# A three-stage kernel: where the decode pieces, the early weight splits and the sums of added tiles stand

## The chip, the cores and the metric

The kernel runs on one core of a Trainium2 chip. The metric is the device time of one launch in microseconds. Engines are named as in the profile: PE (TensorE matmuls), PEld (its weight loads), DVE (VectorE), ACT (ScalarE), POOL (GpSimd), SP (SyncE, used here for transfers). Every engine runs its own list of instructions in order; the order of that list is fixed when the kernel is built.

## What is computed

```python
def _attn_ref(q, k, v):                  # (2, 8, 1152, 64)
    q_pool = q.reshape(B, H, S // 2, 2, D).mean(axis=3)
    scores = np.matmul(q_pool, k.transpose(0, 1, 3, 2)) / np.sqrt(D)
    attn = softmax(scores)
    return np.matmul(attn, v)

def _moe_ref(x, w_gate, w_output_gate, w1, w2):   # x (1152, 512), 8 experts, width 1024
    e_idx = np.argmax(x @ w_gate, axis=1)
    # each token: relu(x @ w1[e]) @ w2[e], scaled by the gate's probability and an output gate

def _moe2_ref(x, w_in, w_out):           # 512 -> 2048 -> 512
    h = x @ w_in
    return (h * np.tanh(softplus(h))) @ w_out
```

The three are applied one after the other to 1152 tokens, all in float32. The weights of the last layer come as 64-bit values (`wio`) that the kernel turns into float32 itself; this is called decoding below.

## The kernel before

**Attention** (stage 1) works on eight pairs of heads, each in nine steps t = 0 to 8, one step per 128 keys. In step t PE makes scores (`sc`, L257 to L268), ACT makes their exponentials `Pt[p, t]` (tile `pt`, 128 x 1152), PE multiplies with the values into the PSUM tile `pvt` (`pv`, L274). The sums of the exponentials, which softmax needs, are also matmuls into `pvt`: `psums` (L284 to L294) multiplies `Pt` by a matrix of ones, `e2`. To halve these, `add_two` (L280) has DVE add the tiles of two steps into `St[p]` (tile `st`): for t in `twos` = (1, 3, 5) it adds Pt[t-1] and Pt[t], and `psums(p, t)` takes `St`. `add_two(p, t-1)` is issued in step t, as its first task, and the values and sums of step t-1 are issued in step t too (the letter p of the string below).

In the same steps PE also makes the score maxima of the *next* pair (`mx`, L215), and DVE reduces them (`Mp`, L103); three PSUM buffers hold them. The order within a step is written out by hand as a string, "0mmrpsmMt": 0 stands for the scores, m and M for one chunk of maxima, p for the values and `psums` of the step before, and so on. Each m first pops one task from a list (`mxc`, L544ff). The tasks are those that a table puts at that step (`at_step`: splitting keys and queries `klo`, `qlo`, the reciprocals `sum_rec`, outputs `x_out`), with `add_two` ahead of all of them, and a decode piece behind. At the end of step 0 ACT and DVE take the sums of the pair before out of PSUM (`post_evac`, tiles `xu` and `sm`), and the next pair's values wait for that, since there is one `pvt`.

**Decoding** (`decode`, L407ff) turns 32 chunks of `wio` (512 KB each, tile `wraw`) into the float32 tiles `wd`. A chunk has three pieces: piece 0 takes an absolute value on ACT (`dm<-wraw`) and a sign on DVE (`ds<-wraw`); piece 1 clamps on DVE (`dm<-dm`) and joins bits (`ds<-wraw,ds`); piece 2 shifts (`dm<-dm`) and writes the result (`wd<-dm,ds`). Pieces are taken strictly in order. Two `wraw` buffers are loaded ahead; the transfers are issued on SP in attention and on ACT afterwards. `DEC_T` says in which steps of pairs 0 to 6 a piece stands, `DEC_A` how many chunks are decoded in attention; in the last pair each step takes up to three pieces. What is left is spread over the iterations of the three wide experts by `DECS`.

**Experts** (stage 2): eight slots in the order of `slots`, three of them wide (ten iterations each), the others narrow (six each); the third wide one is followed by the two last narrow ones. Each iteration splits weights in two parts (`w1h`/`w2h` on ACT, `w1l`/`w2l` on DVE or POOL) and runs matmuls (L826 to L828); a narrow expert runs plain float32 matmuls (L979, L988, L847) with its `xn`, `hr`, `hn` copies on ACT. Results (`y`) are scattered to `ybuf` by POOL (L858). Beside this, `split_hi` (ACT, `wh<-wd`) and `split_lo` (DVE, `wd<-wd,wh`) begin to split the decoded weights of the last layer: `NPRE` of sixteen are done early, the first ones once all chunks are decoded (L1134ff).

**Hand-over**: `reload` (L869) reads three blocks of `ybuf` back by transfers on ACT's queue, which wait for the scatters; `rescale` (L873) multiplies them on DVE; every engine takes a branch (L1161) behind its part; then `turn` (L877, L879) and `add_rows` (L909) bring them to PE for the **last layer** (stage 3).

The last layer's splits are laid out by a table, `stages`: step 0 has `split_hi` of number 3, step 1 its `split_lo`, and so on to number 15.

Of the kernel before, what the change touches and what calls it, by code (L numbers as in the profile page):

```python
# [23 lines left out]
HQ = SQ // 2  # L24
# [6 lines left out]
KT = S // P  # L31
# [53 lines left out]
def kernel(ctx, tc, cst, qt, kt, v, wgo, w1, w2, wio, out):  # L85
    nc = tc.nc
    V, A, G, T, SP = nc.vector, nc.scalar, nc.gpsimd, nc.tensor, nc.sync
    mm = T.matmul
# [4 lines left out]
    def tt(eng, out, a, b, op):  # L93
        eng.tensor_tensor(out=out, in0=a, in1=b, op=op)  # L94
# [53 lines left out]
    e2 = ap.tile([P, 2, 32], F32, name="e2")  # L148
# [8 lines left out]
    Pt, pvt = {}, {}  # L157
# [17 lines left out]
        SP.dma_start(out=vt[p], in_=v[p])  # L175

    DEC_M = 32
    DEC_T, DEC_A = [1, 3, 5, 7, 8], 19
    tqt = {}

    def qsum(p, h):
# [95 lines left out]
    twos = (1, 3, 5)  # L277
    St = {}

    def add_two(p, t):  # L280
        St[p] = ap.tile([P, 2, SQ], F32, name="st", bufs=1)
        tt(V, St[p], Pt[p, t - 1], Pt[p, t], ALU.add)

    def psums(p, t):  # L284


        if t + 1 in twos:
            return
        src = St[p] if t in twos else Pt[p, t]
        for f in range(2):  # L290
            for h in range(2):
                for a in range(2):
                    q_, t0 = 64 * h + 32 * a, 256 * a + 160 * f
                    mm(pvt[p][q_:q_ + 32, f, HQ:HQ + 160], lhsT=e2[:, h], rhs=src[:, h, t0:t0 + 160], start=False, stop=t == KT - 1, skip_group_check=True)  # L294

    def post_evac(p):
        b, hp = divmod(p, 4)
# [102 lines left out]
    dq, wq = [], []  # L400
# [101 lines left out]
    def raw_ahead(pool, end):  # L502
        while dec[2] < min(dec[0] + 2, end):
            load_raw(dec[2], pool)
            dec[2] += 1
# [15 lines left out]
    for g in range(-9, 9 * NPAIR):  # L521
        p, t = divmod(g, 9)
        if t == 0:
            todo = list(chunks) if p + 1 < NPAIR else []
            mtodo = list(mchunks) if p + 1 < NPAIR else []
        tasks = list(sched.get(g, ()))
        if p >= 0 and t - 1 in twos:
            tasks.insert(0, lambda p=p, t=t: add_two(p, t - 1))
        if p == NPAIR - 1:
            tasks.append(lambda: [(raw_ahead(ap, DEC_A), decode_step(ap, DEC_A)) for _ in range(3)])  # L530
        elif p >= 0 and t in DEC_T:
            tasks.append(lambda: (raw_ahead(ap, DEC_A), decode_step(ap, DEC_A)))

        slot = [0]

        def mxc(todo=todo):
            if tasks:
                tasks.pop(0)()
            if todo:
                max_chunk(p + 1, *todo.pop(0))  # L540
            slot[0] += 1

        prev = divmod(g - 1, 9)
        seq = "0mmrpsmMt" if p < NPAIR - 1 else "0mmrpsmmt"
        if g < 0:
            seq = "mmmm"
            todo += mtodo
            mtodo = []
        assert not (t == 8 and (todo or mtodo)), (p, len(todo), len(mtodo))
        if t < 3:  # L550
            seq = seq.replace("M", "m")
        for ch in seq:
            if ch == "0":
                if p >= 0:
                    scores(p, t)
            elif ch == "m":
                mxc()
            elif ch == "M":
                if mtodo:
                    mxc(mtodo)  # L560
                else:
                    mxc()
            elif ch == "s":
                if p > 0 and t == T_S:
                    sum_log(p - 1)
            elif ch == "t":
                if p > 0 and t == T_T:
                    sum_tr(p - 1)
            elif ch == "e":
                mxc([])  # L570
            elif ch == "r":
                if t == 8 and 0 <= p < NPAIR - 1:
                    max_rows(p + 1)
            elif ch in "pfg" and prev[0] >= 0:
                if ch in "pf":
                    pv(*prev, 0)
                if ch in "pg":
                    pv(*prev, 1)
                    psums(*prev)
        for f in tasks:  # L580
            f()
        if t == 0 and p > 0:
            post_evac(p - 1)
        if p > 0 and t in (T_X - 1, T_X):
            x_tr(p - 1, t - T_X + 1)
        if g == -1:
            warm(6)
        if g == -1:
            max_rows(0)
            warm(2)  # L590
# [445 lines left out]
        return [(lambda i=i: pre(i), lambda i=i: main(i), lambda: None) for i in range(-1, 6)]  # L1036

    NF = FF2 // P
    NPRE = 3
    ws2 = {}  # L1040


    def split_hi(b_, f):
        if b_ == 0:
            pool, n = (wq[0], NPRE) if f < NPRE else (zp, NF - NPRE)
            hi = pool.tile([P, 1024], F32R, name="wh", bufs=n)
# [12 lines left out]
    LATE = 1  # L1059
    XGB = 4  # L1060

    DECS = [[0, 0, 0, 0, 0, 0, 0, 0, 2, 2], [0, 2, 2, 2, 2, 2, 2, 2, 2, 2], [0, 2, 2, 2, 2, 2, 2, 2, 2, 1]]
    RQ = 2
    slots = []
    for pos_ in order:
# [31 lines left out]
    for q, (n_, i, _, main, w_, _) in enumerate(flat):  # L1097
        if i == 0:
            used += len(slots[n_][1])
            if n_ + 1 < len(slots):  # L1100
                load_w(slots[n_ + 1][0], ej, slots[n_ + 1][0])
        if q + 2 < len(flat):
            flat[q + 2][2]()
        if gnext < min(used + 4, len(allc)):
            gather(*allc[gnext])
            gnext += 1
        for f in xpre.pop(-q - 1, ()):
            f()
        main()
        if q + 2 < len(flat):  # L1110
            flat[q + 2][5]()
        if q == RQ:
            routing_rest()
            over = routing_over()
        if RQ < q <= RQ + 4:
            oi = next(over)
        if q == RQ + 5:
            routing_oix(oi)
            T.transpose(pr[:TT, P:2 * P], gsc, ident)
            gt_ = rt("gt", [P])  # L1120
            act(gt_[:TT], pr[:TT, P:2 * P])
            A.dma_start(out=gbuf.rearrange("(t p) o -> t (p o)", p=P), in_=gt_[:TT])
            rstack.close()
            fstack = ExitStack()
            fp.append(fstack.enter_context(tc.tile_pool(name="fps", bufs=1, space=PSUM, side="right", reuse_waits="tile")))
            dstack = ExitStack()
            dq.append(dstack.enter_context(tc.tile_pool(name="dq", bufs=1, side="right", reuse_waits="tile")))
            raw_ahead(dq[0], DEC_M)
        if w_ and q > RQ + 5:
            for _ in range(DECS[slots[n_][0]][i]):  # L1130
                decode_step(dq[0], DEC_M)
            raw_ahead(dq[0], DEC_M)
        if dec[0] == DEC_M and dq and not wq:
            dstack.close()
            wq.append(ctx.enter_context(tc.tile_pool(name="wq", bufs=1, side="right", reuse_waits="tile")))
            q0 = q
        elif wq and (q - q0) % 3 == 0 and len(ws2) < NPRE:
            f = len(ws2)
            split_hi(0, f)
            split_lo(0, f)  # L1140
    assert dec[0] == DEC_M and len(ws2) == NPRE, (dec, len(ws2))

# [158 lines left out]
    for i in range(len(steps) + LAG):  # L1301
# [4 lines left out]
        if i < len(steps):  # L1306
            b_, f = steps[i]
# [49 lines left out]
```

## Time and profile before

| | us |
|---|---|
| runs | 706.27, 703.7, 701.53 (median 703.7) |
| profiled execution | 704.62 |
| its span, first to last instruction | 702.6 |
| PE busy in the span | 649.7 (92%) |
| DVE busy | 521.1 (74%) |
| ACT busy | 369.8 (53%) |
| POOL busy | 138.3 (20%) |

Times in rows are microseconds from the start of the span. By stages: attention 0 to 295.4, routing to 314.3, experts to 449.5 (the third wide one's end), the last two narrow experts and the hand-over to 484.4, the last layer to 702.6. A row of a timeline has the start, the duration, engine, line, operation, tiles with their shapes and a count; in brackets the idle time of the engine just before it and what released it. An L number is a line of the kernel, and where a helper issues all operations (L91, L94, L97, L100, L103) the tile names tell them apart.

### The profile page before, as it was taken

To read this page: it belongs to the slowest core of one execution; us is meant where nothing else is said; L and a number is where in the kernel's file an instruction comes from. 1 tells how busy PE (TensorE), PEld (TensorE's weight loads), DVE (VectorE), ACT (ScalarE), POOL (GpSimd) and SP (SyncE) were. 2 spreads that over 40 slices of the span, in tenths; PEclk is the share of its full clock that TensorE was granted. 3 is DMA by queue.
4 is the path that set the end of the run, shared out by engine and by line. 5 is a ranking of instruction groups with operands and counts; after the bars stand their busy time and mean duration, and the time that the engine had idled before them with its cause. 6 is when DMAs were issued, how large, how long until landed. Compare 5 with 4: busy or idle time off the path is not lost. (4 is left out here: it accounts for less than half of the span.)

```text
span 702.6 us, 11490 instructions
## 1 busy us (share of the span) xinstructions
PE 649.7 (92%) x4335; PEld 503.0 (72%) x4335; DVE 521.1 (74%) x1034; ACT 369.8 (53%) x752; POOL 138.3 (20%) x139
## 2 busy tenths in 40 slices
PE   4999999999999999859989999968899999999997
PEld 3766767666667666438877968638787899999995
DVE  6896969787787978556554848732999977897775
ACT  6556575656565646324245535433666554555543
POOL 5300000000000000034023323201322332233322
PEclk9999999999999999979999999998999999999999
DMA  6854544344442113158489778851000020001001
GB/s 226 281 144 119 132 131 112 114 114 130 114 132 84 64 47 131 41 163 327 172 309 354 263 261 315 302 209 46 0 1 1 1 91 1 0 1 46 1 0 45
DMA packets 26641, 88.33 MB, mean 126 GB/s; under 512 B 2886, under 2 KB 7631, under 8 KB 22482
## 3 DMA queue, kind: packets, MB, share of 16 engines
q1 hardware_dynamic: 20688, 71.13, 29.2%
q0 software_dynamic: 3568, 8.79, 5.6%
q10 hardware_dynamic: 2322, 7.61, 3.1%
q8 instruction: 35, 0.57, 0.3%
q14 instruction: 28, 0.23, 0.1%
HBM read 79.65 MB, written 8.39 MB: 125 GB/s over the span
## 5 line engine op out<-in xcount | busy, mean ns | idle before, releaser
L91 ACT ACTIVATE pt<-sc 128x320 f32<-128x320 f32 (+1 forms) x216 | 96.5, 488 | 66.9 <-PE sc L259 59.8
L103 DVE TENSOR_REDUCE Mp<-mx 128x1 f32<-128x384 f32 x198 | 102.9, 548 | 37.4 <-PE mx L215 36.3
L100 POOL TENSOR_SCALAR u<-u 128x384 f32<-128x384 f32 x48 | 60.6, 1263 | 153.1 <-ACT u L91 132.3
L274 PE MATMUL pv<-pt,vt 128*64 128x288 f32 x576 | 86.8, 422 | 1.0 <-DVE sm L94 0.5
L215 PE MATMUL mx<-at,qs 128*128 128x384 f32 x176 | 57.3, 383 | 10.4 <-DVE qs L97 8.4
L826 PE MATMUL zps<-yh,wh 128*128 128x384 f32 x188 | 64.0, 341 | 1.7 <-DVE n L97 1.7
L828 PE MATMUL zps<-yl,wh 128*128 128x384 f32 x188 | 63.3, 337 | 0.0
L827 PE MATMUL zps<-yh,wd 128*128 128x384 f32 x180 | 60.8, 338 | 0.0
L1266 PE MATMUL ops<-wh,gl 128*128 128x512 f32 x144 | 57.7, 403 | 3.0 <-DVE gl L94 2.4
L274 PEld LDWEIGHTS pv<-pt,vt 128*64 128x64 f32 x576 | 35.7, 137 | 31.8 <-issue 15.1
L1266 PE MATMUL ops<-wh,gh 128*128 128x512 f32 x144 | 56.9, 395 | 0.2 <-ACT gh L91 0.2
L215 PEld LDWEIGHTS mx<-at,qs 128*128 128x128 f32 x176 | 31.3, 195 | 31.1 <-issue 11.3
L1266 PE MATMUL ops<-wd,gh 128*128 128x512 f32 x135 | 53.1, 394 | 0.0
L91 ACT ACTIVATE l<-n,two 128x384 f32<-128x384 f32 x48 | 29.5, 615 | 25.0 <-DVE n L97 25.0
L97 DVE SCALAR_TENSOR_TENSOR l<-n,r 128x384 f32<-128x384 f32 x48 | 26.6, 555 | 19.1 <-ACT r L91 19.1
L91 ACT ACTIVATE u<-zps 128x384 f32<-128x384 f32 x48 | 23.2, 484 | 33.1 <-PE zps L828 29.7
L826 PEld LDWEIGHTS zps<-yh,wh 128*128 128x128 f32 x188 | 35.4, 188 | 3.7 <-ACT r L91 2.0
L1266 PEld LDWEIGHTS ops<-wh,gl 128*128 128x128 f32 x144 | 27.0, 188 | 14.0 <-DVE gl L94 7.0
L91 ACT ACTIVATE gh<-n 128x384 fp32r<-128x384 f32 x48 | 24.8, 517 | 20.6 <-DVE n L97 20.4
L828 PEld LDWEIGHTS zps<-yl,wh 128*128 128x128 f32 x188 | 35.3, 188 | 0.0
L100 DVE TENSOR_SCALAR dm<-dm 128x512 f32<-128x512 f32 x64 | 29.7, 464 | 7.4 <-ACT dm L91 7.3
L91 ACT ACTIVATE dm<-wraw 128x512 f32<-128x512 f32 x32 | 21.7, 678 | 25.0 <-DMA wraw<-in_wio 17.0
(276 smaller groups left out, 1593.0 us busy)
## 6 DMA issues: line engine op xcount, KB each, us to landing
wt<-in_w SPq DMA_DIRECT2D x32, 1024.0 KB, 7.1
wraw<-in_wio SPq DMA_DIRECT2D x19, 512.0 KB, 4.7
kd<-in_kt SPq DMA_DIRECT2D x16, 576.0 KB, 3.8
wraw<-in_wio ACTq DMA_DIRECT2D x13, 512.0 KB, 6.9
vt<-in_v SPq DMA_DIRECT2D x8, 576.0 KB, 7.1
tq<-in_qt SPq DMA_DIRECT2D x12, 288.0 KB, 6.3
tq<-in_qt POOLq DMA_DIRECT2D x12, 288.0 KB, 4.5
pt<-in_qt SPq DMA_DIRECT2D x4, 576.0 KB, 3.9
```

The source lines that it names most:

```text
L91: A.activation(out=out, in_=in_, func=func, **kw)
L97: V.scalar_tensor_tensor(out=out, in0=a, scalar=s, in1=b, op0=op0, op1=op1)
L100: eng.tensor_scalar(out=out, in0=a, scalar1=s1, scalar2=s2, op0=op0, op1=op1)
L103: V.tensor_reduce(out=out, in_=in_, axis=AX.X, op=op)
L215: mm(ps[:, :384], lhsT=QS[p, h][:, j * P:(j + 1) * P], rhs=At[p, h][:, cs_], start=True, stop=True)
L274: mm(pvt[p][64 * h:64 * h + 64, f, :HQ], lhsT=vt[p][:, t, h, :], rhs=Pt[p, t][:, h, f * HQ:(f + 1) * HQ], start=t == 0, stop=t == KT - 1, ...
L826: mm(out_, lhsT=a, rhs=c, start=first, stop=False)
L827: mm(out_, lhsT=b_, rhs=c, start=False, stop=False)
L828: mm(out_, lhsT=a, rhs=d, start=False, stop=last_)
L1266: mm(opt[b_, j], lhsT=(g_, g_, gl_)[i], rhs=(wo, wl_, wo)[i], start=f == 0 and i == 0, stop=f == NF - 1 and i == 2)
```

## The change

Four numbers or rules change.

1. `add_two(p, t-1)` is the third task of step t instead of the first, so it stands behind the split and decode work of that step. `psums` takes `St` one step later: where t-1 is in `twos`, `psums(p, t)` multiplies `St` (and then, if t is not part of a sum of two, `Pt[p, t]`).
2. `DEC_T` gets step 0: six pieces per pair instead of five. `DEC_A` is 23 instead of 19. Pairs 0 to 6 hold 42 pieces instead of 35, and the last pair all 27 instead of 22.
3. `DECS`: the first wide expert keeps its four pieces, the second takes 20 (18 before), the third 3, in its first three iterations (17 before, in iterations 1 to 9).
4. `NPRE` is 4, and early splits come every second iteration from the end of the decoding, not every third. The table `stages` is not changed, so split number 3 is issued early and again in the last layer.

```diff
-    DEC_T, DEC_A = [1, 3, 5, 7, 8], 19
+    DEC_T, DEC_A = [0, 1, 3, 5, 7, 8], 23
...
     def psums(p, t):
-        if t + 1 in twos:
-            return
-        src = St[p] if t in twos else Pt[p, t]
-        for f in range(2):
-            for h in range(2):
-                for a in range(2):
-                    q_, t0 = 64 * h + 32 * a, 256 * a + 160 * f
-                    mm(pvt[p][q_:q_ + 32, f, HQ:HQ + 160], lhsT=e2[:, h], rhs=src[:, h, t0:t0 + 160], start=False, stop=t == KT - 1, skip_group_check=True)
+        for src in ([St[p]] if t - 1 in twos else []) + ([] if t in twos or t + 1 in twos else [Pt[p, t]]):
+            for f in range(2):
+                for h in range(2):
+                    for a in range(2):
+                        q_, t0 = 64 * h + 32 * a, 256 * a + 160 * f
+                        mm(pvt[p][q_:q_ + 32, f, HQ:HQ + 160], lhsT=e2[:, h], rhs=src[:, h, t0:t0 + 160], start=False, stop=src is Pt.get((p, KT - 1)), skip_group_check=True)
...
         if p >= 0 and t - 1 in twos:
-            tasks.insert(0, lambda p=p, t=t: add_two(p, t - 1))
+            tasks += [lambda: None] * (2 - len(tasks))
+            tasks.insert(2, lambda p=p, t=t: add_two(p, t - 1))
...
-    NPRE = 3
+    NPRE = 4
...
-    DECS = [[0, 0, 0, 0, 0, 0, 0, 0, 2, 2], [0, 2, 2, 2, 2, 2, 2, 2, 2, 2], [0, 2, 2, 2, 2, 2, 2, 2, 2, 1]]
+    DECS = [[0] * 8 + [2, 2], [2] * 10, [1] * 3 + [0] * 7]
...
-        elif wq and (q - q0) % 3 == 0 and len(ws2) < NPRE:
+        elif wq and (q - q0) % 2 == 0 and len(ws2) < NPRE:
```

Two places show how this moves instructions. The first is DVE in steps 1 to 3 of pair 2 (`Bt` is a key split, `qs` a query split, `sm` the sums of the pair before). Before:

```order
L94 TENSOR_TENSOR Bt_112<-kd,at 64x576
L103 TENSOR_REDUCE Mp_117<-mx 128x1 x2
L100 TENSOR_SCALAR dm<-dm 128x512
L97 SCALAR_TENSOR_TENSOR ds<-wraw,ds 128x512
L103 TENSOR_REDUCE Mp_117<-mx 128x1
L94 TENSOR_TENSOR st<-pt 128x1152
L103 TENSOR_REDUCE Mp_117<-mx 128x1
L97 SCALAR_TENSOR_TENSOR qs<-tq,qs 64x576
L103 TENSOR_REDUCE Mp_117<-mx 128x1 x3
L94 TENSOR_TENSOR Bt_113<-kd,at 64x576
```

With the change, from the same place on:

```order
L94 TENSOR_TENSOR Bt_112<-kd,at 64x576
L103 TENSOR_REDUCE Mp_117<-mx 128x1 x2
L100 TENSOR_SCALAR dm<-dm 128x512
L97 SCALAR_TENSOR_TENSOR ds<-wraw,ds 128x512
L103 TENSOR_REDUCE Mp_117<-mx 128x1
L97 SCALAR_TENSOR_TENSOR qs<-tq,qs 64x576
L103 TENSOR_REDUCE Mp_117<-mx 128x1 x2
L94 TENSOR_TENSOR st<-pt 128x1152
L103 TENSOR_REDUCE Mp_117<-mx 128x1 x2
L94 TENSOR_TENSOR Bt_113<-kd,at 64x576
```

`st` moved behind the query split and two of the reductions, and ahead of `st` the next pair's maxima are reduced earlier. The same instructions are there.

The second place is ACT from the third wide expert's last iteration through the two narrow experts to the hand-over (`dm` is a decode piece, `wh` an early split, `hr`, `hn`, `xn` and the `xh` from `yp` belong to the narrow experts, L869 is `reload`). Before:

```order
L91 ACTIVATE dm<-wraw 128x512
L91 ACTIVATE y<-yp 128x512 x2
L91 ACTIVATE hr<-hps 128x256
L91 ACTIVATE hn<-hps 128x256
L91 ACTIVATE hr<-hps 128x256
L91 ACTIVATE hn<-hps 128x256
L91 ACTIVATE wh<-wd 128x1024
L91 ACTIVATE xn<-xps 128x4x64
L91 ACTIVATE xh<-yp 64x256 x2
L91 ACTIVATE wh<-wd 128x1024
L91 ACTIVATE hr<-hps 128x256
L869 DMA xl<-ybuf 128x512 x3
```

With the change:

```order
L91 ACTIVATE wh<-wd 128x1024
L91 ACTIVATE y<-yp 128x512 x2
L91 ACTIVATE hr<-hps 128x256
L91 ACTIVATE wh<-wd 128x1024
L91 ACTIVATE hn<-hps 128x256
L91 ACTIVATE hr<-hps 128x256
L91 ACTIVATE hn<-hps 128x256
L91 ACTIVATE xn<-xps 128x4x64
L91 ACTIVATE xh<-yp 64x256 x2
L91 ACTIVATE hr<-hps 128x256
L868 DMA xl<-ybuf 128x512 x3
```

The decode piece ahead of `y` is gone and an early split stands there, whose input was decoded many iterations before. The last early split stands behind the first `hr`; the two further back, and a third one behind `reload`, are gone from this stretch.

## Rows read from the trace of the kernel before

**Rows 1.** Windows, whole core, one row a stretch: us, busy (count) per engine PE, PEld, DVE, ACT, POOL, PEclk, DMA share, GB/s.

```profile
0.00:295.40 295.40, 277.20 (x2288) 189.38 (x2288) 235.73 (x482) 175.96 (x375) 26.42 (x44) 0.99 0.43 126
...
449.50:484.40 34.90, 24.68 (x192) 17.04 (x192) 11.45 (x26) 11.20 (x24) 4.25 (x5) 0.95 0.55 193
```

**Rows 2.** Waits: engine, line, waited for: us in total, times, longest.

```profile
PE pv L294 <- DVE st L94: 4.9, 8, 2.0
```

**Rows 3.** Timeline, PE, pair 2: start us, us, operation, count, [idle before <- releaser].

```profile
100.86 0.75 PE L294 MATMUL pv<-st,e 128*32 128x160 f32 x16 [0.65 <-DVE st L94]
...
102.71 0.45 PE L215 MATMUL mx<-at,qs 128*128 128x384 f32 x1 [0.20 <-DVE Mp L103]
```

**Rows 4.** Windows, as in 1: pair 2's steps 0 and 1 to 6, the last pair, its low clock.

```profile
90.40:94.30 3.90, 3.90 (x41) 2.75 (x38) 1.02 (x3) 3.41 (x8) 0.00 (x0) 1.00 0.02 4
94.30:118.83 24.53, 23.61 (x188) 16.54 (x187) 23.42 (x48) 13.45 (x29) 1.95 (x3) 1.00 0.50 139
264.50:289.24 24.74, 21.67 (x188) 13.96 (x176) 23.31 (x50) 14.63 (x31) 0.24 (x1) 0.95 0.32 107
286.60:290.00 3.40, 3.40 (x21) 1.71 (x23) 2.84 (x7) 1.35 (x3) 0.00 (x0) 0.51 0.18 50
```

**Rows 5.** Lines with forms apart, DVE, attention: count, busy us, mean ns, idle before.

```profile
L94 DVE TENSOR_TENSOR st<-pt 128x1152 f32<-128x1152 f32 x24 | 32.3, 1346 | 0.0
...
L97 DVE SCALAR_TENSOR_TENSOR wd<-dm,ds 128x512 int32<-128x512 int32 x19 | 13.2, 693 | 0.7
L97 DVE SCALAR_TENSOR_TENSOR ds<-wraw,ds 128x512 int32<-128x512 int32 x19 | 12.9, 681 | 0.0
...
L100 DVE TENSOR_SCALAR ds<-wraw 128x512 int32<-128x512 int32 x19 | 8.0, 421 | 0.3
```

**Rows 6.** Timeline, PE, step 6 of the last pair.

```profile
285.12 0.75 PE L294 MATMUL pv<-st,e 128*32 128x160 f32 x16 [1.98 <-DVE st L94]
```

**Rows 7.** Timeline, DVE, then POOL, third wide expert.

```profile
433.39 1.52 DVE L100 TENSOR_SCALAR dm<-dm 128x512 f32<-128x512 f32 x1
...
433.15 1.48 POOL L94 TENSOR_TENSOR w1l<-wt,w1h 128x512 fp32r<-128x512 f32 x1 [0.57 <-DVE w2l L94]
```

**Rows 8.** Timeline, PE, first matmuls of iterations, third wide expert.

```profile
432.50 0.28 PE L826 MATMUL hps<-xh,w1h 128*128 128x256 f32 x1
...
435.90 0.39 PE L826 MATMUL hps<-xh,w1h 128*128 128x256 f32 x1 [0.30 <-DVE hl L97]
...
438.83 0.28 PE L826 MATMUL hps<-xh,w1h 128*128 128x256 f32 x1
...
445.93 0.39 PE L826 MATMUL yp<-w2h,hh 128*128 128x512 f32 x1
```

**Rows 9.** Timeline, ACT, the last two narrow experts.

```profile
451.50 0.69 ACT L91 ACTIVATE dm<-wraw 128x512 f32<-128x512 f32 x1 [4.08 <-DMA wraw<-in_wio]
...
462.44 1.93 ACTq L869 DMA_DIRECT2D xl<-ybuf  x3
464.48 0.38 ACT L91 ACTIVATE hn<-hps 128x256 f32<-128x256 f32 x1 [2.95 <-DMA ybuf<-y,six]
...
466.75 1.05 ACT L91 ACTIVATE wh<-wd 128x1024 fp32r<-128x1024 f32 x1
```

**Rows 10.** Timeline, POOL, then DVE, then PE, the same stretch.

```profile
454.44 0.98 POOL L858 DMA_INDIRECT ybuf<-y,six  x1 [0.30 <-ACT hn L91]
...
467.82 1.23 DVE L94 TENSOR_TENSOR wd<-wd,wh 128x1024 fp32r<-128x1024 f32 x1 [5.50 <-ACT wh L91]
...
470.39 1.46 DVE L100 TENSOR_SCALAR xl<-xl,gsc 128x512 f32<-128x512 f32 x3
...
464.92 1.08 PE L847 MATMUL yp<-wt,hn 128*64 128x256 f32 x8 [1.64 <-ACT hn L91]
...
471.10 0.38 PE L877 MATMUL yb<-tri,zero 128*128 128x512 f16 x1 [1.99 <-PEq L1161]
474.63 1.65 PE L879 MATMUL yb<-cs,xl 128*128 128x128 f32 x6 [3.15 <-DVEq L1161]
```

## The prediction

> **What bounds the kernel now.** I read the windows by stage first, then the waits, then timelines of the places where they lie. In attention PE is busy for 277.20 of 295.40 us, in the stretch of the last narrow experts and the hand-over for only 24.68 of 34.90 [rows 1]. The change touches three places: the pairs of heads, the third wide expert, and that last stretch.
>
> In a pair of heads two engines are full. In steps 1 to 6 of pair 2 PE works 23.61 us of 24.53 and DVE 23.42 [rows 4]: the stretch can be no shorter than DVE's work, and 1.11 us is all that is between them. Step 0 is the other way round: DVE works 1.02 us of 3.90 there, and PE all of it [rows 4]. PE waits for `st`, the sums of two tiles, 4.9 us in eight waits over all pairs [rows 2]. One of them is in step 2 of pair 2: 0.65 us, with another 0.20 for a reduction behind it [rows 3]; the longest, 1.98 us, is in the last pair [rows 6]. Behind it the granted clock is 0.51 for 3.40 us [rows 4], the lower of the two levels, 1.2 GHz where it is 2.4 otherwise.
>
> In the third wide expert PE has small stalls behind DVE's decode pieces [rows 7, 8]. In the last stretch PE waits for ACT and for DVE in turn. The head of the chain is the last decode piece: ACT stands 4.08 us for its transfer until 451.50, and the results `y` of the wide expert, next on ACT, stand behind it [rows 9]. So the scatter on POOL is late [rows 10], so is the reload at 462.44, and `hn` behind the reload [rows 9]. PE waits for that `hn` 1.64 us, and at the end 3.15 us for DVE's branch, since DVE does a weight split at 467.82 (which it waited 5.50 us for) and the rescaling at 470.39 before [rows 10].
>
> **Part 1, the sums of two tiles.** `st` takes 1.346 us each, 24 of them [rows 5]; their number and the matmuls stay. What moves is the order on DVE. PE's wait of 0.65 us in pair 2 goes, since the sum now has a whole step's time. But PE is also fed by DVE's reductions, with three PSUM buffers between them, and all of DVE's work in steps 1 to 6 is still there. I laid out DVE's rows of pair 2 in the new order with their durations: the maxima in step 2 come 1.3 us earlier, and PE then waits some 0.4 us at step 3 and twice 0.3 us in step 5, where the sum now stands ahead of a reduction. Of 0.85 us [rows 3] about 0.1 is left. The bounds per pair are a gain of 1.11 us (DVE without any gap [rows 4]) and a loss of about as much (the sum, 1.346 us [rows 5], in front of a reduction that PE waits for, where PE has almost no lead).
>
> **Part 2, the sixth piece.** A piece is on DVE 0.42 us (piece 0), or 0.42 and 0.68 (piece 1), or 0.42 and 0.69 (piece 2) [rows 5], the clamp and the shift taken like the sign. The new one in step 0 is piece 0, 0.42 us on DVE beside an activation on ACT, in the step where DVE has 2.88 us free [rows 4]. It stands ahead of `sm`, which the next pair's values wait for: I take 0.25 us of it as felt. The transfers (512 KB a chunk on SP) run where the share of the transfer engines is 0.02 to 0.50 [rows 4]; hidden. In pairs 3 and 6 step 1 had the short piece 0 and now has piece 1, 0.68 more, a loss in pair 3; pair 6 has piece 2 one step away from the place where it hurt. Over pairs 1 to 6 I sum to **-0.4 us** (bounds: -5 and +6, at a gain of 0.85 or a loss of 1.0 in each of six). Pair 0, whose DVE is full from its start, gets the longer piece in step 1: **+0.5**.
>
> The last pair is full: DVE works 23.31 us of 24.74 [rows 4], and 27 pieces stand there rather than 22. Ahead of the third sum there are three more pieces, together 0.42 + 0.42 + 0.68 + 0.42 + 0.69 = 2.63 us [rows 5], and an output copy; and in each step piece 1 now follows piece 0 at once, and so waits for ACT's `dm`, which stands behind the exponentials. The sum, ready before at 285.1 [rows 6], is ready at about 289.8. PE comes to it one step later, at about 287, and waits 2.7 us instead of 1.98. From there PE has the work that lay between 285.12 and 295.4 less a step: 10.3, less 1.7 that the low clock cost (half of 3.40 [rows 4]), less 3.1, is 5.5, which gives 295.3 without a low clock and 297.0 with it. The old wait had the low clock behind it, and the new one is longer: **+1.7** (bounds 0 and +2.4).
>
> **Part 3, DECS.** The second wide expert gets two more pieces in its first iteration, 0.42 + 0.42 + 0.68 at most, where DVE had gaps; PE had no stall there that came from DVE. I take 0, with +1 as its bad end: a clamp that took 1.52 us in the third one, when it began inside a POOL split of 1.48 us [rows 7], takes 0.42 elsewhere [rows 5].
>
> The Trainium skill, "SBUF — State Buffer", in "Who interferes with whom", says that the port pair DVE shares with GpSimd is an exclusive lock, so that a two-port operation of DVE and a GpSimd operation block each other whole. Rows 7 agree: 1.52 is what is left of the POOL split and 0.4. By that rule the sum would be up to 2.2 us worse in the second wide expert (two clamps at 1.52 in place of 0.42) and 1.1 better in the third.
>
> The third wide expert loses 14 pieces from iterations 3 to 9. Its iteration from 435.90 to 438.83 takes 2.93 us, the one before 3.40, where a reduction of the hidden layer stood behind pieces [rows 8]. From 432.50 to 445.93 are four iterations, 13.43 us [rows 8], against 4 x 2.83 = 11.3 at the pace of its best ones; some of the 2.1 is the next expert's tokens, and the last two iterations have about 0.7 of their own. The early splits take their place (1.05 us on ACT [rows 9], 1.23 on DVE [rows 10], one in two iterations), less than the pieces. I take **-2.0** (bounds -1.0 and -2.4).
>
> **Part 4, early splits and the last stretch.** With no decode piece on ACT, `y` starts when PE's result is there, about 1.1 us after the wide expert's end (449.46) rather than at 452.1: 1.5 us earlier, and scatter and reload with it. The reload starts 8.0 us after the second scatter [rows 9, 10]; two early splits on ACT (1.05 each) have also left the way to it. PE's wait of 1.64 for `hn` falls to about 0.6, and one of 1.2 us for the first `hr`, behind `y`, goes. So PE ends its narrow experts about 2.2 us earlier. The split on DVE ahead of the rescaling is gone, and DVE's rescaling, bound now only by the reload, ends some 16.3 us after the wide expert rather than 22.4. Then PE no longer waits for DVE: of its 3.53 us from its own branch at 471.10 to 474.63 [rows 10] all is free. 2.2 + 3.5 = 5.7; I take **-5.5** (bounds -3.0, if the reload's transfers land late, and -6.5 with a shorter low clock behind a shorter wait). Split number 3 is done early, but the last layer's table does it again: 1.05 on ACT and 1.23 on DVE at its first steps, as before, so the fourth early split buys nothing there. Last layer: 0.
>
> **Sum.** +0.5 - 0.4 + 1.7 - 2.0 - 5.5 = -5.7. The profiled execution took 704.62, its span 702.6; it is 0.9 above the median of 703.7, so the sum against it is 698.9 (span 696.9), against the median 698.0.
>
> **Rivals.**
> (a) *The sums' waits come back whole.* If PE's three buffers carry it over the sums, the 4.9 us of [rows 2] go and with them the low clock of the last pair (1.7): 703.7 - 4.9 - 1.7 + 0.5 - 2.0 - 5.5 = 690.1. For it: those waits have one releaser. Against: DVE is full over steps 1 to 6, and in the last pair more so.
> (b) *The last stretch gives little.* If the reload's landing, or PE's own branch with the low clock, sets the end, 3.0 instead of 5.5, and the third wide expert 1.0 instead of 2.0: 698.0 + 3.5 = 701.5. For it: `hn` waited for the reload's transfers, and that wait may stay [rows 9]. Against: all that is ahead of them moves 1.5 us or more.
> (c) *Slower: the pairs pay for the sixth piece.* If `sm`, and with it the values of the next pair, stand behind the new piece while that waits for ACT's `dm` or its transfer, PE waits about 1.3 us in each of pairs 1 to 7: +9.1 on 698.0, less the 0.25 a pair already in it: 705.4. It decides against the rest from about 1.05 us a pair. For it: PE has 3.90 busy of 3.90 in step 0 and nothing to spare; DVE in order. Against: DVE has 2.88 us free there [rows 4].
> (d) *Nothing changes in total.* Parts may cancel, 702 to 705; it lies within (b) and (c).
>
> **How the numbers follow.** My forecast has 0.50 with its own range 695.5 to 700.5, (a) 0.17, (b) 0.20, (c) 0.13. The range that leaves out half of (a)'s cases and half of (c)'s reaches from 691.0 to 705.0. A measurement of this kernel can tell about 1%, 7 us, from no change. Faster than 696.7 are (a) and about a third of my forecast's cases: 0.33. Slower than 710.7 needs (c) at twice its price or the last pair worse too: 0.05. Same: 0.62.
>
> **What would show it.** In the profile of the changed kernel the wait of PE for `st` in steps of pairs 1 to 6 should be gone, with waits for reductions (`Mp`) in its place, and the pairs' length within 0.5 us of before. In the last pair PE's wait for the third sum should be 2 to 3 us, with the low clock behind it, and the stage's end near 297. The third wide expert should take 23.5 us rather than 25.6, ACT's 4.08 before `y` be gone, PE's wait for DVE's branch near 0, and the span from the wide expert's end to the first `yb` about 19.6 rather than 25.2. Two activations should write `wh` from the same `wd`. Wrong would be: pairs that change by a microsecond each in either direction, or a last stretch that keeps its length.

## The result, and the profile after

The changed kernel takes 696.9 us (median of 8 runs, 693.93 to 699.65) against 703.74 us (8 runs, 701.04 to 706.68). The ratio is 0.991, with an interval of 0.9886 to 0.9939: 4.3 to 8.0 us faster. The forecast was 698.0 in a range of 691.0 to 705.0.

The total came out; its parts did not all. The table gives each stretch, in us, in the profiled executions, from PE's own start times (a pair from its first scores to the next pair's, the last pair to the product with `xu`; the last stretch from the third wide expert's end to the first product with the reloaded rows).

| stretch | before | after | difference | forecast |
|---|---|---|---|---|
| up to pair 0 | 24.78 | 23.16 | -1.6 | 0 |
| pair 0 | 31.59 | 33.90 | +2.3 | +0.5 |
| pairs 1 to 6 | 205.43 | 206.58 | +1.2 | -0.4 |
| last pair | 34.43 | 32.26 | -2.2 | +1.7 |
| routing, to the first tokens | 15.10 | 16.06 | +1.0 | 0 |
| first experts | 58.32 | 57.83 | -0.5 | 0 |
| second wide expert and the narrow one before it | 43.64 | 43.64 | 0 | 0 |
| narrow expert behind it | 10.60 | 9.27 | -1.3 | 0 |
| third wide expert | 25.58 | 24.80 | -0.8 | -2.0 |
| last stretch | 25.17 | 19.82 | -5.4 | -5.5 |
| turn and last layer | 227.97 | 228.07 | +0.1 | 0 |
| span | 702.60 | 695.38 | -7.2 | -5.7 |

Three rows are mostly chance: the two of pair 0 and the first experts. Five kernels run below share pair 0's code with one of these two: with the code of before it took 31.59, 35.51 and 33.68 us, with that of after 33.90, 31.84, 34.21 and 32.72. The time up to it moves too. The first experts took 53.4 to 59.2 us in kernels with the same code there. Pairs 1 to 6 do repeat: 205.39 to 205.44 us in three executions with the code of before, 206.42 to 206.58 in four with that of after. The third wide expert took 25.58, 25.91 and 26.85 us with the pieces of before and 24.16 to 25.86 in seven kernels with the three of after, so its -0.8 is known only roughly. The last stretch took 24.45 to 25.84 before (three executions) and 18.72 to 20.11 in seven kernels with those three pieces.

**Pairs.** PE's timeline, pair 2 of the changed kernel (start us, us, operation, idle before and releaser):

```profile
97.13 1.19 PE L274 MATMUL pv<-pt,vt 128*64 128x288 f32 x8 [0.42 <-PE mx L215]
...
104.48 0.44 PE L215 MATMUL mx<-at,qs 128*128 128x384 f32 x1 [0.21 <-DVE Mp L103]
```

The wait for `st` of [rows 3] is gone; 0.42 us stands ahead of the values in step 1 and 0.21 in step 3. The waits view of the whole kernel, with PEld's and PE's waits, shows where the rest went. First the kernel before, then after:

```profile
PEld pv L294 <- DVE st L94: 12.7, 16, 2.5
...
PEld mx L215 <- DVE Mp L103: 6.0, 14, 0.6
```

```profile
PEld mx L215 <- DVE Mp L103: 18.9, 39, 1.7
...
PE mx L215 <- DVE Mp L103: 3.5, 8, 1.5
...
PEld pv L292 <- DVE st L94: 2.5, 2, 2.1
PE pv L292 <- DVE st L94: 1.6, 1, 1.6
```

Weight loads waited 12.7 us for `st` and now wait 2.5; for the reductions `Mp` they waited 6.0 and now wait 18.9. They run beside the matmuls, so this is not PE's time: PE itself waits 1.6 us for `st` (4.9 in [rows 2]) and 3.5 for `Mp` (2.0 before). DVE was nearly full in steps 1 to 6, as [rows 4] had it, and is so still. The windows of the changed kernel are step 0 and steps 1 to 6 of pair 2, then a place in the last pair (us, busy of PE, PEld, DVE, ACT, POOL, PEclk, DMA share, GB/s):

```profile
91.25:95.13 3.88, 3.88 (x40) 2.73 (x37) 1.02 (x2) 3.17 (x8) 0.00 (x0) 1.00 0.09 26
95.13:118.46 23.33, 22.60 (x166) 15.44 (x166) 22.33 (x48) 13.68 (x29) 2.15 (x3) 1.00 0.56 150
...
286.60:290.00 3.40, 1.84 (x39) 1.08 (x34) 3.37 (x6) 0.77 (x3) 0.00 (x0) 1.00 0.45 154
```

DVE works 22.33 of 23.33 us, PE 22.60. The window of [rows 4] for these steps reaches 0.75 us into step 7; from score product to score product, as here, they took 23.81 us before, with DVE at 22.86. The third line is the place in the last pair where the clock was 0.51 in [rows 4]; now it is 1.00.

**The last pair and routing.** PE, then DVE, then ACT of the changed kernel:

```profile
269.04 1.19 PE L274 MATMUL pv<-pt,vt 128*64 128x288 f32 x8 [1.00 <-DVE sm L94]
...
288.89 0.75 PE L292 MATMUL pv<-st,e 128*32 128x160 f32 x16 [1.56 <-DVE st L94]
...
297.55 0.87 PE L319 MATMUL mx<-cs,sm 128*128 128x128 f32 x3 [0.92 <-DVE sm L94]
```

```profile
287.48 1.35 DVE L94 TENSOR_TENSOR st<-pt 128x1152 f32<-128x1152 f32 x1
...
296.92 0.48 DVE L94 TENSOR_TENSOR sm<-pv,sm 64x320 f32<-64x320 f32 x1
...
294.06 0.71 ACT L91 ACTIVATE dm<-wraw 128x512 f32<-128x512 f32 x1 [1.78 <-DMA wraw<-in_wio]
```

PE waits 1.00 us for `sm` and 1.56 for the third sum; before, it waited 0.54 for `sm` and 0.28, 0.27 and 1.98 [rows 6] for the three sums. At the end the last decode piece stands on ACT for its transfer (1.78 us), so the pieces end at 296.9 on DVE, `sm` behind them, and PE waits 0.92 for it.

**The last stretch.** ACT, DVE and PE of the changed kernel:

```profile
446.92 1.28 ACT L91 ACTIVATE y<-yp 128x512 f32<-128x512 f32 x2 [1.57 <-PE yp L827]
...
449.77 1.05 ACT L91 ACTIVATE wh<-wd 128x1024 fp32r<-128x1024 f32 x1
...
458.04 1.30 ACTq L868 DMA_DIRECT2D xl<-ybuf  x3
...
462.43 1.07 DVE L100 TENSOR_SCALAR xl<-xl,gsc 128x512 f32<-128x512 f32 x2 [4.10 <-PE yp L846]
...
466.44 0.38 PE L876 MATMUL yb<-tri,zero 128*128 128x512 f16 x1 [2.36 <-PEq L1160]
467.31 1.26 PE L878 MATMUL yb<-cs,xl 128*128 128x128 f32 x8 [0.50 <-DVEq L1160]
```

`y` starts at 446.92, before the wide expert's end (447.49), not 2.6 us behind it; the reload stands 10.6 us behind the end (13.0 in [rows 9]), `hn` no longer waits for it, and PE's wait for DVE's branch is 0.50 us (3.15 in [rows 10]).

### The profile page after: what moved, and what is told of

Read it like the earlier page. It is cut to its first block, busy times and chain, and to the rows that moved or that the text cites. A ratio compares the mean times of both kernels' runs of the same rounds, so it can differ in the third digit from the quotient of the medians.

```text
span 695.4 us, 11495 instructions
## 1 busy us (share of the span) xinstructions
PE 649.5 (93%) x4335; PEld 503.6 (72%) x4335; DVE 523.1 (75%) x1035; ACT 370.8 (53%) x753; POOL 140.1 (20%) x139
## 5 line engine op out<-in xcount | busy, mean ns | idle before, releaser
L215 PE MATMUL mx<-at,qs 128*128 128x384 f32 x176 | 60.9, 392 | 11.4 <-DVE qs L97 7.1
L274 PEld LDWEIGHTS pv<-pt,vt 128*64 128x64 f32 x576 | 35.5, 136 | 32.6 <-issue 13.6
L215 PEld LDWEIGHTS mx<-at,qs 128*128 128x128 f32 x176 | 31.8, 194 | 36.3 <-DVE Mp L103 18.9
L826 PEld LDWEIGHTS zps<-yh,wd 128*128 128x128 f32 x180 | 34.1, 189 | 1.5
```

The lines of the kernel that those rows point to most:

```text
L215: mm(ps[:, :384], lhsT=QS[p, h][:, j * P:(j + 1) * P], rhs=At[p, h][:, cs_], start=True, stop=True)
L274: mm(pvt[p][64 * h:64 * h + 64, f, :HQ], lhsT=vt[p][:, t, h, :], rhs=Pt[p, t][:, h, f * HQ:(f + 1) * HQ], start=t == 0, stop=t == KT - 1, ...
L826: mm(out_, lhsT=b_, rhs=c, start=False, stop=False)
```

## The experiments

Each ratio is to runs of the kernel before made with it.

**1. The sums alone.**

```diff
 # against the kernel before
+            tasks += [lambda: None] * (2 - len(tasks))
+            tasks.insert(2, lambda p=p, t=t: add_two(p, t - 1))   # and psums a step later
```

> The kernel before with the sums of two tiles alone taken a step later (third task of the step, psums a step later); pieces, DECS and early splits as before. My theory (DVE is full in steps 1 to 6 of a pair, so the wait for st is only exchanged for waits on reductions): pairs 1 to 6, 205.4 us before, take 204.6 to 205.6; in the last pair, with 22 pieces, the wait of 1.98 us goes and the low clock behind it too, 2 to 4 us; the rest is unchanged; median 700 to 702. Rival (the waits for st come back whole): pairs 1 to 6 take 203 us or less, median 697. Second rival (the sums' move is worth nothing by itself, the last pair too): 703.5.

Measured: 699.73 us, ratio 0.9967 (0.9941 to 0.9994). Pairs 1 to 6 took 203.82 us, 1.6 less than before, which lies between my theory (204.6 or more) and the rival (203 or less); the last pair took 31.00 with its wait for the third sum at 0.76:

```profile
283.63 0.75 PE L292 MATMUL pv<-st,e 128*32 128x160 f32 x16 [0.76 <-DVE st L94]
```

So moving the sums wins 0.27 us a pair, and 3.4 us in the last pair, where PE's waits for `sm` and the sums fall from 3.07 us to 1.30 and the low clock did not come.

**2. All but the sums.**

```diff
 # against the changed kernel
-            tasks.insert(2, lambda p=p, t=t: add_two(p, t - 1))
+            tasks.insert(0, lambda p=p, t=t: add_two(p, t - 1))   # and psums as before
```

> The changed kernel with the sums taken as before (first task of the step), all else of the change kept. My theory: pairs 1 to 6 take 205.5 to 207.5 us (the wait for st is back, the sixth piece stands in step 0), the last pair, with 27 pieces, waits 2 to 3 us for the third sum and has the low clock behind it; experts and last stretch as in the changed kernel; median 698 to 701. Rival (the move of the sums is what makes room for the sixth piece): pairs 1 to 6 take 210 us or more, median 704. Second rival (the move does nothing): 697.

Measured: 697.57 us, ratio 0.9938 (0.9903 to 0.9973). Pairs 1 to 6 took 208.05, 2.6 more than before and 1.5 more than in the changed kernel, and just above the 207.5 I had allowed; the rival that asked for 210 falls. The last pair took 34.56, with 0.66, 1.31 and 1.73 us of waits for its three sums, shorter than the 2 to 3 us I expected, and no low clock. The median alone does not rule out the second rival (697, the move does nothing); these two stretches, 1.5 and 2.3 us longer than in the changed kernel, speak against it. The third wide expert (24.63) and the last stretch (18.91) are as in the changed kernel.

**3. Early splits as before.**

```diff
 # against the changed kernel
-    NPRE = 4
+    NPRE = 3
-        elif wq and (q - q0) % 2 == 0 and len(ws2) < NPRE:
+        elif wq and (q - q0) % 3 == 0 and len(ws2) < NPRE:
```

> The changed kernel with three early splits, one in three iterations, as before. My theory (the last stretch became shorter because no decode piece stands ahead of the wide expert's results on ACT): the stretch from the third wide expert's end to the first product with the reloaded rows stays within 1 us of the changed kernel's 20 us; median 696 to 698. Rival (the gain came from the splits leaving the path to the hand-over): the stretch is 22.5 us or longer, median 699.5 or more.

Measured: 695.59 us, ratio 0.9904 (0.987 to 0.9938). The last stretch is 18.84 us. The rival falls: three splits, one of them inside the stretch, lose nothing.

**4. Five pieces per pair.**

```diff
 # against the changed kernel
-    DEC_T, DEC_A = [0, 1, 3, 5, 7, 8], 23
+    DEC_T, DEC_A = [1, 3, 5, 7, 8], 20
-    DECS = [[0] * 8 + [2, 2], [2] * 10, [1] * 3 + [0] * 7]
+    DECS = [[0] * 8 + [2, 2], [2] * 10, [2] * 6 + [0] * 4]
```

> The changed kernel with five pieces per pair (none in step 0), 20 chunks in attention, and 12 pieces in the first six iterations of the third wide expert, none in its last four. My theory: pair 0 gets 1 to 2 us shorter than in the changed kernel and the last pair about 1 us, pairs 1 to 6 are within 1 us in sum; the third wide expert loses 0.5 to 1.5 us; the last stretch keeps its gain, since its head is free of pieces; median 695 to 698. Rival (the gain of the last stretch needs the third wide expert free of pieces as a whole, since the early splits come later): the stretch is 2 us or more longer, median 699 to 700.

Measured: 695.95 us, ratio 0.99 (0.9864 to 0.9935). The last stretch keeps its gain (20.34 us), as expected. Four sizes were missed: pair 0 (34.35 us) and the last pair (32.24) did not get shorter; pairs 1 to 6 took 203.85 us, the same as in experiment 1, so the sixth piece, with the other pieces that it shifts, costs 2.7 us in the changed kernel; and the third wide expert took 27.92, 3.1 more. The last two about cancel.

**5. Split number 3 once.**

```diff
 # against the changed kernel
     def split_hi(b_, f):
-        if b_ == 0:
+        if b_ == 0 and f not in ws2:
...
-        if b_ == 0:
+        if b_ == 0 and len(ws2[f]) == 1:
```

> The changed kernel with split number 3 done once, early, and left out of the last layer's table. My theory (the second one lies beside PE's work): the last layer, 218.15 us in the changed kernel (216.6 where no low clock falls in it), stays within 0.2 us of one of these two, the turn before it the same; median as the changed kernel's, 695 to 698. Rival (the repeated split delays the layer's first steps by its 1.05 us on ACT): the stage from the first product with the reloaded rows to the end gets 1 us shorter.

Measured: 695.94 us, ratio 0.9923 (0.9887 to 0.9959); the last layer took 218.13 us against 218.15. The repeated split costs nothing. In the last pair PE waited 2.59 us for the third sum here, since a piece stood for its transfer, with no low clock.

**6. The piece of step 0 behind `sm`.**

```diff
 # against the changed kernel
...
             post_evac(p - 1)
+        if t == 0:
+            for f in late:      # the pieces of step 0, no longer among the tasks
+                f()
```

> The changed kernel with the pieces of step 0 issued behind the taking out of the sums of the pair before (behind xu and sm on ACT, behind sm on DVE), not ahead of it. Theory A (the sixth piece costs by standing ahead of xu and sm on ACT): step 1 of pairs 1 to 5 goes from 3.58 back to 3.24 us, pairs 1 to 6 take 204.6 us (206.6 in the changed kernel), the last pair 0.4 less; 2.4 us in all; median 694 to 695. Theory B (it costs by its DVE time in the full steps that follow): pairs 1 to 6 stay at 206 to 207, since what step 1 wins comes back as waits for reductions in steps 2 to 5.

Measured: 695.48 us, ratio 0.9909 (0.988 to 0.9938). In pairs 2 to 5, step 1 went from 3.58 to 3.24 us as theory A has it, but step 3 grew from 4.42 to 4.61: pairs 1 to 6 took 206.13, 0.45 less than in the changed kernel, where A asked for 2.0. Theory B holds for most of it; where the 0.34 in step 1 comes from is taken up below. The last pair took 35.92 us here, with the case I had forecast in it:

```profile
289.75 0.75 PE L292 MATMUL pv<-st,e 128*32 128x160 f32 x16 [2.63 <-DVE st L94]
```

```profile
291.20:294.60 3.40, 3.40 (x18) 2.49 (x16) 3.30 (x8) 1.36 (x3) 0.00 (x0) 0.50 0.68 205
```

**7. The kernel before, its last pieces one iteration earlier.**

```diff
 # against the kernel before
-    DECS = [..., [0, 2, 2, 2, 2, 2, 2, 2, 2, 1]]
+    DECS = [..., [2, 2, 2, 2, 2, 2, 2, 2, 1, 0]]
```

> The kernel before with the 17 pieces of the third wide expert one iteration earlier (none in its last one): the last transfer of a chunk starts and lands some 2.8 us earlier, so ACT does not stand in front of y; the pieces, the instructions and three early splits remain, the splits one iteration earlier too. My theory (y, the scatters and the reload were late because ACT waited for that transfer): the stretch from the third wide expert's end to the first product with the reloaded rows falls from 25.2 to 22.0 to 23.7 us; median 701 to 702.5 against 703. Rival (the piece's mere presence, or the early splits' place, is what counts): it stays at 24.7 or longer.

Measured: 698.11 us, ratio 0.9959 (0.9919 to 0.9998). The last stretch fell to 20.24 us, more than I expected. ACT, DVE and PE:

```profile
447.20 0.67 ACT L91 ACTIVATE dm<-wraw 128x512 f32<-128x512 f32 x1 [2.19 <-DMA wraw<-in_wio]
448.87 1.29 ACT L91 ACTIVATE y<-yp 128x512 f32<-128x512 f32 x2 [1.00 <-PE yp L828]
...
463.46 1.23 DVE L94 TENSOR_TENSOR wd<-wd,wh 128x1024 fp32r<-128x1024 f32 x1 [5.56 <-ACT wh L91]
...
469.69 1.16 PE L879 MATMUL yb<-cs,xl 128*128 128x128 f32 x8 [0.55 <-DVEq L1161]
```

The piece still stands ahead of `y` and still waits for its transfer (2.19 us), but it is done before PE's result is there; `y` then waits for PE alone. The split on DVE ahead of the rescaling is there too (463.46) and costs nothing. So nearly the whole gain of the last stretch, 4.9 us of the 5.4 (4.2 against the second execution of the kernel before, 24.45), comes from the transfer that ended last. The pieces cost more where they went: the third wide expert took 28.52.

**8. The kernel before, again.**

> The kernel before once more, for a second profile. If the low clock of 3.4 us behind the wait of 1.98 us in the last pair follows from that wait, it is there again and the last pair takes 34.4 us from its first scores to the product with xu; if it fell there by chance, the wait is there and the pair takes 32.7. The pairs 1 to 6 should take 205.4 again within 0.2, pair 0 between 31 and 34 by the arrival of its inputs.

```profile
287.82 0.75 PE L294 MATMUL pv<-st,e 128*32 128x160 f32 x16 [1.97 <-DVE st L94]
```

```profile
289.30:292.70 3.40, 3.40 (x23) 2.19 (x26) 2.83 (x7) 1.36 (x3) 0.00 (x0) 0.62 0.17 50
```

Measured, in one run of 706.67 us: the same wait (1.97) and a low clock behind it, the last pair 34.41 us, pairs 1 to 6 205.44 us, pair 0 35.51, above what I expected. In experiment 7, which has the same attention, it took 34.39.

**9. The last pair without its third sum of two.**

```diff
 # against the changed kernel, in psums and at add_two
+        tw = twos[:2] if p == NPAIR - 1 else twos
```

> The changed kernel without the third sum of two tiles in the last pair (its two tiles go to PE one by one: 16 more matmuls, 0.75 us, and 1.35 us less on DVE). My theory (in the last pair DVE's pieces and the waits of ACT and of transfers ahead of them set when the third sum is ready, PE waits 1.56 to 2.6 us there in four kernels of this order, and a low clock follows in some): the wait and the low clock go, the last pair takes 31.3 to 31.8 us (32.3, 32.3, 33.3 and 35.9 so far); median 1 to 2 us below the changed kernel's 696.9. Rival (the pair's end is set by the exponentials or by the pieces themselves): 32.3 or more again, no gain.

Measured: 692.46 us, ratio 0.9889 (0.9848 to 0.9929). The last pair took 31.31 us, as my theory has it, and the clock stayed high.

**10. Experiments 6 and 9 together.**

> The run before it, and the pieces of step 0 behind xu and sm as well. From the run with that alone: 0.45 us less in pairs 1 to 6, the last pair's wait for sm 0.54 in place of 1.0, the routing stage 15.3 in place of 16.1. Last pair 30.8 to 31.4; 1 to 1.5 us below the run before it if the parts add, the same if the routing's 0.75 comes back elsewhere.

Measured: 691.63 us, ratio 0.9867 (0.9827 to 0.9907). Pairs 1 to 6 took 206.25, the last pair 31.28, the routing 16.50, where I expected 15.3. It is the fastest of the kernels run, but its interval overlaps those of experiment 9 and of the changed kernel, so only that it beats the kernel before is shown.

**11. No pieces in the third wide expert.**

```diff
 # against the kernel of experiment 10
-    DECS = [[0] * 8 + [2, 2], [2] * 10, [1] * 3 + [0] * 7]
+    DECS = [[0] * 8 + [2, 2], [3] + [2] * 7 + [3, 3], [0] * 10]
```

> The run before it, with the last three pieces in the second wide expert (23 there, none in the third), so the early splits fall into the narrow expert between the two. Theory A (the stall of 1.07 us in the third wide expert comes from pieces on DVE that meet POOL's weight splits): the third wide expert takes 23.5 to 24.0 us in place of 24.8 to 25.3, the second one stays at 43.6, the narrow one grows by 0 to 1 us by the splits on ACT. Theory B (the stall comes from POOL's late weight splits alone): the third stays at 24.8.

Measured: 695.87 us, ratio 0.9921 (0.9889 to 0.9952). The third wide expert took 24.56 us, 1.30 less than the 25.86 of experiment 10 but above theory A's 24.0; the narrow expert grew by 0.84. PE's wait for `hl` is what A said would go. First experiment 10, then this run:

```profile
431.50 0.39 PE L830 MATMUL hps<-xh,w1h 128*128 128x256 f32 x1 [1.07 <-DVE hl L97]
```

```profile
424.70 0.39 PE L830 MATMUL hps<-xh,w1h 128*128 128x256 f32 x1 [0.29 <-DVE hl L97]
```

So the wait of 1.07 us goes with the pieces, as A has it. The time follows less well: part of it is a new wait of 0.44 us, for a `w1l` that stands on DVE behind an early split, and the stretch varies by over 1 us between executions anyway. The median is 4.2 us above that of experiment 10, though these two stretches together got 0.5 us shorter; why is open. DVE and POOL still slow each other (POOL, then DVE):

```profile
426.89 5.49 POOL L94 TENSOR_TENSOR w1l<-wt,w1h 128x512 fp32r<-128x512 f32 x3 [1.09 <-ACT w1h L91]
...
424.56 1.79 DVE L94 TENSOR_TENSOR w2l<-wt,w2h 128x512 fp32r<-128x512 f32 x1
...
426.61 0.68 DVE L94 TENSOR_TENSOR w2l<-wt,w2h 128x512 fp32r<-128x512 f32 x1
427.21 2.31 DVE L94 TENSOR_TENSOR wd<-wd,wh 128x1024 fp32r<-128x1024 f32 x1
429.45 0.41 DVE L97 SCALAR_TENSOR_TENSOR hl<-hps,hh 128x256 fp32r<-128x256 f32 x1
...
431.49 1.44 DVE L94 TENSOR_TENSOR w2l<-wt,w2h 128x512 fp32r<-128x512 f32 x1
```

With no decode piece left, three of the weight splits `w2l` take 1.44 to 1.79 us instead of 0.68 while POOL splits `w1l`, and an early split 2.31 instead of 1.23 [rows 10].

## Why the forecast held, and where its steps did not

**The last stretch: right in size.** Forecast -5.5, measured -5.4. The working named the transfer that ACT stood for, and experiment 7 shows that this alone brings 4.9. Its two terms were 2.2 us for PE's earlier end of the narrow experts and 3.5 for its time from its branch to the reloaded rows. They measured 3.1 and 2.3 (2.7 less behind the branch, 0.4 more ahead of it), so the sum came out closer than its parts. Two of its steps were wrong. `y` came 3.2 us earlier, not 1.5. And I gave the DVE split ahead of the rescaling a share; in experiment 7 it is there and the stretch is 20.24 us. Rival (b), a small gain because the reload lands late, falls: `hn` does not wait for it any more.

**Pairs 1 to 6: the sign was wrong.** Forecast -0.4, measured +1.2. The first step that failed is the adding up: 0.1 us won and 0.25 lost in each of six pairs, and a loss in pair 3, give +0.9 or more, not -0.4. To get -0.4, the sums of two must win 0.35 a pair; they win 0.27 (experiment 1). That DVE's full steps give the waits back as waits for reductions was right in part only. In pairs 1 to 6 PE's own waits for `st` are 2.2 of the 4.9 us, and experiment 1 won 1.6. For the sums alone, rival (a) was nearer to this than the 0.1 a pair of part 1; for the whole change it falls, 690.1 against 696.9.

The sixth piece, with the pieces that it shifts, costs 0.46 a pair (206.58 against 203.85 in experiment 4). Step by step this is 0.33 to 0.35 in step 1 of each of pairs 1 to 5, nothing there in pair 6, and in pair 3, where the prediction saw a loss, another 0.7 in steps 2, 3 and 5; the other 0.3 us is spread over the pairs. So "I take 0.25 us of it as felt" was near (0.28 on average in step 1), but its ground, 2.88 us free on DVE in step 0, does not hold where the piece stands. DVE, then ACT, of pair 2 of the changed kernel, then DVE of pair 6:

```profile
95.16 0.56 DVE L103 TENSOR_REDUCE Mp<-mx 128x1 f32<-128x384 f32 x1 [1.33 <-PE mx L215]
95.63 0.42 DVE L100 TENSOR_SCALAR ds<-wraw 128x512 int32<-128x512 int32 x1
95.97 0.55 DVE L103 TENSOR_REDUCE Mp<-mx 128x1 f32<-128x384 f32 x1
96.55 0.48 DVE L94 TENSOR_TENSOR sm<-pv,sm 64x320 f32<-64x320 f32 x1
```

```profile
95.66 0.43 ACT L91 ACTIVATE sm<-pv 64x320 f32<-64x320 f32 x1
```

```profile
231.36 0.42 DVE L100 TENSOR_SCALAR ds<-wraw 128x512 int32<-128x512 int32 x1
232.77 1.02 DVE L103 TENSOR_REDUCE Mp<-mx 128x1 f32<-128x384 f32 x2 [0.99 <-PE mx L215]
233.82 0.48 DVE L94 TENSOR_TENSOR sm<-pv,sm 64x320 f32<-64x320 f32 x1
```

In pair 2, and alike in pairs 1 and 3 to 5, DVE's idle time lies ahead of a reduction that waits for PE (1.33 us), and `ds` of the new piece stands behind that reduction. So it delays the next reduction and `sm`, for which the values wait. ACT's part of `sm` ended at 96.09, 0.46 us before DVE came to it, so the piece's activation on ACT is not the cause. In pair 6 ACT has that activation at the same place, but `ds` stands ahead of both reductions, in the idle time, and step 1 takes 3.24 us as without the piece. Experiment 6, with `ds` behind `sm`, won 0.34 in step 1 and lost 0.2 in step 3: the DVE time is felt there too. To put `ds` ahead of both reductions in all pairs was not tried. Rival (c), more than 1.05 us a pair, falls too.

**The last pair: the term failed.** Forecast +1.7, measured -2.2. I had the third sum ready 28.0 us behind the pair's start (289.8); it was 25.2, against 23.3 before. The step that failed is "ahead of the third sum there are three more pieces": there are none. Eighteen stand ahead of it before and after; the five added ones all come behind it. On DVE of the changed kernel:

```profile
269.88 0.43 DVE L100 TENSOR_SCALAR dm<-dm 128x512 f32<-128x512 f32 x1 [0.44 <-ACT dm L91]
...
274.35 0.43 DVE L100 TENSOR_SCALAR dm<-dm 128x512 f32<-128x512 f32 x1 [0.77 <-ACT dm L91]
...
286.88 0.69 DVE L94 TENSOR_TENSOR xr<-mx,rc 128x512 f32<-128x512 f32 x1
```

What made it 1.9 us later is the output copy `xr` (0.69), two waits for ACT's `dm` (0.44 and 0.77) and a `sm` that comes 0.46 later behind a piece 2, less some 0.4 won back between. PE waited 1.56 us, and the low clock, which I added, did not come. PE's waits for `sm` and the sums fell from 3.07 us to 2.56, and the low clock had cost 1.7: together that is the -2.2. How often the low clock comes is open. In the kernel before it followed a wait of 1.97 to 1.98 us in three executions of three; in the changed order it followed one of 2.63 (experiment 6), but not 2.59 (experiment 5) and 1.96 (experiment 4). So the length of that wait alone does not decide it, and what does was not tried. In three executions with the changed attention code it did not come, and the pair took 32.26, 32.28 (experiment 3) and 33.28 us (experiment 5): a gain of 1.1 to 2.2 repeats, but that the 1.7 of the clock belongs to the new order is not shown.

**Routing and the third wide expert: two costs too small.** The routing was taken as untouched, and lost 1.0: the last piece's transfer is late, `sm` stands behind the pieces, and PE waits 0.92 us for it. In the third wide expert I forecast -2.0, at least -1.0, and got -0.8 in these two executions. In the changed kernel (PE, then DVE, then POOL):

```profile
432.72 0.39 PE L825 MATMUL hps<-xh,w1h 128*128 128x256 f32 x1 [1.07 <-DVE hl L97]
...
429.12 1.52 DVE L100 TENSOR_SCALAR dm<-dm 128x512 f32<-128x512 f32 x1
430.56 1.78 DVE L97 SCALAR_TENSOR_TENSOR ds<-wraw,ds 128x512 int32<-128x512 int32 x1
...
427.34 6.13 POOL L94 TENSOR_TENSOR w1l<-wt,w1h 128x512 fp32r<-128x512 f32 x4 [2.52 <-PE hps L827]
```

A clamp and a join take 3.3 us instead of 1.1 beside four POOL splits, and PE waits 1.07 for `hl` behind them. I had seen one such row [rows 7], and counted on its going with the pieces; three pieces were left, and one of them met POOL's splits. Without the three the wait goes, but experiment 11 shows that the expert's own splits are stretched in the same way. The Trainium skill, "SBUF — State Buffer", "Who interferes with whom", says that a DVE instruction with two inputs in SBUF contends with a GpSimd instruction that reads SBUF. The rows of experiment 11 agree: `w2l`, with two inputs in SBUF, takes 1.44 to 1.79, and `hl`, which reads one of its two from PSUM, 0.41 in the same stretch. For the clamp, the prediction's reading of [rows 7] is only rough: 1.24 us were left of the POOL split, which with the clamp's usual 0.42 is 1.66, not 1.52. The loss of up to 2.2 us that it priced for the second wide expert did not come (43.64 us in every run).

**The narrow expert behind the second wide one: not in the sum.** It won 1.3 us (0.7 to 1.3 against the four executions with the pieces of before, 9.98 to 10.60 us). Before, a piece stood on ACT ahead of `hr` (ACT, then PE, of the kernel before):

```profile
416.35 0.68 ACT L91 ACTIVATE dm<-wraw 128x512 f32<-128x512 f32 x1 [2.36 <-issue]
...
416.92 0.38 ACT L91 ACTIVATE hr<-hps 128x256 f32<-128x256 f32 x1
...
417.35 0.44 PE L988 MATMUL hps<-cs,hr 128*128 128x128 f32 x2 [1.26 <-ACT hr L91]
```

In the second execution of the kernel before (experiment 8) the profile names the transfer, so this is the mechanism of the last stretch:

```profile
419.33 0.68 ACT L91 ACTIVATE dm<-wraw 128x512 f32<-128x512 f32 x1 [1.84 <-DMA wraw<-in_wio]
```

In the changed kernel `hr` starts at 415.42, 2.0 us behind the narrow expert's start, not 3.6. I had looked at the second wide expert's PE waits and not at what stands behind its last pieces.

**Nothing from the fourth early split.** As forecast: neither doing it (experiment 3 without it is as fast) nor repeating it (experiment 5) moves the time.

So the total held because errors cancel: pairs 1 to 6 (+1.6), routing (+1.0) and the third wide expert (+1.2) came out worse than forecast, the last pair (-3.9) and the narrow expert (-1.3) better; part of the third wide expert's share is chance, and the clock's 1.7 in the last pair may be. What carries the result is the last stretch.

## What to carry to other kernels

Look for work that waits for a transfer in the in-order list of an engine that also hands over results: what the row behind it waits for is the whole price, and in that stretch moving the transfer one iteration earlier was worth nearly as much as taking the work away. Where an engine is full over a stretch, a wait removed there comes back in another place, at least in part. Idle time of an in-order engine is free only for work that stands ahead of what the engine idles for: the sixth piece stood behind it in five pairs and cost 0.33 us in each, and ahead of it in one and cost nothing in its step. Sum a change stage by stage against the profile, since a total that holds can hide terms that cancel.

## What was not expected

- The same attention code took 31.6 to 35.5 us in pair 0 and the first experts 53.4 to 59.2, in single executions: differences of 2 us there say nothing without a second profile.
- A low clock follows PE's idle time of about 2 us in some executions and not in others (above).
- DVE and POOL slowed each other down by up to 1.1 us an instruction in a stretch without any decode piece.
